# The second and third head pair turned by another engine, with a new start order, and a reordered last stage, in a kernel of attention and two expert layers

## The chip, the core and the metric

The kernel runs on one core of a Trainium2 chip. Its engines each work through a queue of their own and wait for each other through semaphores: TensorE (PE in the profile; its weight loads are PEld), VectorE (DVE), ScalarE (ACT), GpSimd (POOL) and SyncE (SP), which here issues DMAs. The metric is the device time of one execution in microseconds (us), the median of three runs.

## The reference

The kernel computes attention with a memory term, then a layer with x - tanh(x), then a layer with a softmax gate and a layer normalisation:

```
q, k, v: (4, 8, 576, 64)    M_prev: (4, 8, 64, 64)    z_prev: (4, 8, 64)    beta: (8)
scores = q @ k.T / 8, causal;  a = exp(scores - max) / (sum + 1e-9);  local = a @ v
q_p = where(q > 0, q, exp(q) - 1) + 1
mem = (q_p @ M_prev) / (q_p . z_prev + 1e-6)
x = sigmoid(beta) * mem + (1 - sigmoid(beta)) * local        -> (2304 tokens, 512)

h = x @ w_in (512 x 2048);  y = (h - tanh(h)) @ w_out

h = y @ w2_in (512 x 1024);  e = exp(h - max(h));  u = h * e / (sum(e) + 1e-9)
out = ((u - mean(u)) / sqrt(var(u) + 1e-6) * g_ln) @ w2_out  -> (2304, 512)
```

## The kernel before

**Attention.** The 32 heads are worked on in 16 pairs, the two heads of a pair in the lower and upper 64 partitions. For each pair q and k come from memory as rows of tokens and have to be turned, so that the 64 features lie on partitions. There are two ways. `load_n` (L183) fetches them in natural layout, `t_pe` (L203) turns them with 18 small matmuls on TensorE, and `t_cp` (L213) copies the result out of PSUM, on ScalarE for q and on VectorE for k. Or `_load` (L159) fetches each of them in four overlapping pieces of 32 partitions by 1120 numbers, and `q_t`, `k_t` (L241) turn them with one VectorE instruction (L245). The first three pairs (0 to 2) go the first way, all later ones the second.

With q and k turned, `s_r` (L303) computes the scores of a pair block by block, and `s_l` (L328) the scores of the last 64 tokens of two pairs together (S_L, issued with the odd pair). VectorE adds the mask and takes the maximum (`s_max`, L345, which appears as L353), ScalarE takes the exponential with its sum (`s_exp`), GpSimd scales (`s_norm`, L407), TensorE turns the probabilities (`a_t`), and `a_pv` multiplies by v into the PSUM tile X, which `a_mem` (L429) has opened with the memory term. The memory term itself takes `f_neg`, `f_exp`, `f_max` (the function of q) and `m_mm` (L279), `m_eps`, `m_inv`, `m_mul`. `g_exp`, `g_inv` (L119 to L121) compute the gate from beta.

The order of all these steps at the start is a table written out by hand, `PROLOGUE` (L516): each entry is a step, its pair, the engine (s SyncE, a ScalarE, v VectorE, p GpSimd) and a part; `run` (L579) issues them in that order. From pair 4 on `PERIOD` takes over, a table for two pairs. Since an engine works through its queue in order, the table's order is the order of each queue.

PSUM is shared: tag S has two tiles of 1024 columns in turn (scores, S_L, the memory product R, turned q and k, later H), T two of 512, X one.

**The two layers.** The first (Moe1) runs from about 190 to 590 us, with steps h and y alternating on TensorE. The second (Moe2) works on 18 blocks of 128 tokens, 0 to 17, in the loop at L1214. For block i:

- `y_split` (L1245): the block's y is split into a high half (ScalarE, L1246) and a low half (GpSimd, L1247) for products of full precision.
- `h_mm` (L919): H = y @ w2_in, 24 matmuls of 512 columns on TensorE.
- `top` (L930): the row maximum on VectorE. `exp` (L936): the exponential on ScalarE.
- `norm`: on VectorE L944 to L950 (sum, product, mean and variance), then the power -1/2 of the variance on GpSimd (L951), then the normalisation on VectorE (L958).
- `turn` (L960): blocks 1 to 16 are turned in 32x32 squares by VectorE (L964), written to memory (L966) and read back in four pieces (L969); this is the round trip. Blocks 0 and 17 are turned by TensorE instead (`t_parts`, L986, with the high half on ScalarE at L996 and the low half on VectorE at L1001).
- `spread` (L974): what came back is split into a high half (ScalarE, L979) and a low half (GpSimd, L980).
- `o_mm` (L1003): the product with w2_out, 24 matmuls, into PSUM tag X (blocks 0 to 14 and 16), S (15) or both (17); the products with the high half come first, those with the low half last. Then a copy out of PSUM on ScalarE (L1018) and the store. A tile O1X in the profile is the product of block 1 in tag X: it can start when O0X, in the same PSUM tile, has been copied out.

The loop issues `h_mm(i)` and the other steps of block i, and `o_mm(i - 3)` at its end. As the code stands there is an order by hand here too:

```
m2.h_mm(i); m2.y_split(i + 2); m2.top(i); m2.exp(i)
if i > 3: m2.spread(i - 2)
m2.norm(i); next(lo, None)          # lo: the low halves of block 0, at i == 1
if i == 3: m2.spread(1)
m2.turn(i)
if i > 2: m2.o_mm(i - 3)
```

Of the kernel before, what the change touches and what calls it, by code (L numbers as in the profile page):

```python
# [31 lines left out]
class Attention:  # L32
# [150 lines left out]
    def load_n(self, p, k):  # L183

        D, src = self.D, (self.q, self.k)[k]
        b, h0 = divmod(2 * p, self.H)
        if p == 1:
            t = self.ap.tile([P, self.poff[self.NC - 1]], F32, tag="P", name=f"N{p}_{k}", bufs=4)
        else:
            t = self.sp.tile([P, self.S * 2], F32, tag="nqnk"[2 * k : 2 * k + 2], name=f"N{p}_{k}", bufs=1)  # L190
# [325 lines left out]
    PROLOGUE = """  # L516
        load_n:0:s:0 load_n:0:a:1 load_v:0:s warm:0:- heat:0:-:8 load_g:0:- load_n:1:s:1
        t_pe:0:-:0 t_cp:0:a:0 load_n:1:s:0 f_neg:0:p load_m:0:- t_pe:0:-:1 t_cp:0:v:1 g_exp:0:-
        s_r:0:-:2 f_exp:0:- g_inv:0:- w_ld:2:- s_max:0:-:4 m_gate:0:- s_r:0:-:1 load_n:2:s:1
        s_exp:0:-:4 s_max:0:-:0 s_r:0:-:3 s_max:0:-:5 load_n:2:s:0 s_exp:0:-:5 s_max:0:-:7  # L520
        t_pe:1:-:0 s_exp:0:-:0 s_max:0:-:6 s_exp:0:-:7 t_pe:1:-:1 s_max:0:-:2 g_cpy:0:-
        s_exp:0:-:2 s_max:0:-:1 t_cp:1:v:1 t_cp:1:a:0 f_neg:1:p s_l:1:- s_exp:0:-:1 s_max:0:-:3
        s_exp:0:-:3 f_max:0:- s_exp:0:-:6 s_max:1:-:8 s_r:1:-:1 s_eps:0:-:1 s_exp:1:-:8
        s_eps:0:-:0 s_inv:0:-:1 s_norm:0:-:5 s_r:1:-:3 s_inv:0:-:0 s_max:1:-:9 f_exp:1:-
        s_norm:0:-:0 s_max:1:-:6 t_pe:2:-:0 load_q:3:s s_norm:0:-:4 s_exp:1:-:9 s_max:1:-:7
        s_norm:0:-:3 t_cp:2:a:0 s_r:1:-:2 s_max:1:-:1 s_max:1:-:3 s_norm:0:-:6 s_max:1:-:2
        s_exp:1:-:6 s_max:1:-:0 m_mm:0:- s_norm:0:-:2 s_max:1:-:5 s_exp:1:-:7 s_max:1:-:4
        s_norm:0:-:7 s_exp:1:-:0 a_t:0:-:0 m_eps:0:- f_max:1:- s_eps:1:-:0 s_exp:1:-:5
        t_pe:2:-:1 load_k:3:s m_inv:0:- a_ev:0:a:0 s_inv:1:-:0 s_norm:1:-:8 m_mul:0:-
        s_exp:1:-:4 a_t:0:-:4 a_ev:0:v:4 a_t:0:-:2 a_ev:0:a:2 s_norm:0:-:1 a_t:0:-:5  # L530
        s_norm:1:-:9 t_cp:2:v:1 a_t:0:-:1 a_ev:0:a:5 load_v:1:s s_norm:1:-:7 a_t:0:-:3
        a_ev:0:a:3 a_t:0:-:6 f_neg:2:p s_r:2:-:3 s_max:2:-:7 a_ev:0:a:6 s_exp:1:-:1 m_mm:1:-
        a_ev:0:a:1 f_exp:2:- s_max:2:-:6 s_r:2:-:1 s_exp:1:-:2 m_eps:1:- f_max:2:- s_exp:1:-:3
        s_eps:1:-:1 s_r:2:-:2 s_max:2:-:2 s_exp:2:-:7 s_max:2:-:1 a_mem:0:- s_inv:1:-:1
        s_norm:1:-:5 m_inv:1:- s_exp:2:-:2 s_max:2:-:3 a_pv:0:-:0 s_max:2:-:5 s_exp:2:-:5
        s_norm:1:-:1 s_max:2:-:4 s_norm:1:-:4 a_pv:0:-:1 s_max:2:-:0 m_mul:1:- s_exp:2:-:4
        s_norm:1:-:3 a_pv:0:-:3 s_exp:2:-:3 q_t:3:- s_norm:1:-:2 a_pv:0:-:2 s_exp:2:-:6
        s_norm:1:-:0 a_t:1:-:1 a_ev:1:a:1 x_ev:0:v s_norm:1:-:6 a_t:1:-:3 m_mm:2:- f_neg:3:p
        a_ev:1:a:3 k_t:3:- s_exp:2:-:1 a_t:1:-:0 s_exp:2:-:0 m_eps:2:- a_t:1:-:2 m_inv:2:-
        a_ev:1:a:0 m_mul:2:- s_eps:2:-:0 a_mem:1:- s_eps:2:-:1 a_ev:1:a:2 s_inv:2:-:0  # L540
        s_norm:2:-:7 a_t:1:-:4 s_inv:2:-:1 a_ev:1:a:4 s_l:3:- s_max:3:-:8 s_r:3:-:1 s_r:3:-:3
    """


# [733 lines left out]
```

## Time and profile before

| what | value |
| --- | --- |
| median of three runs | 799.09 us (798.41, 799.12, 799.09) |
| the profiled execution | 798.38 us |
| its span (first to last instruction) | 796.3 us |
| granted TensorE clock | 1.00 throughout |
| TensorE busy, share of the span | 783.3 us, 98% |
| weight loads | 698.5 us, 88% |
| VectorE | 571.1 us, 72% |
| ScalarE | 353.3 us, 44% |
| GpSimd | 373.6 us, 47% |

A share is a mean over stages. The same sums over a stretch show which engine is full there, and the timeline of an engine shows its groups of instructions in order, with the idle time ahead of a group and what ended it in square brackets.

### The profile page before, as it was taken

What the parts mean: (1) busy time and instruction counts of PE and PEld (TensorE: products, weight loads), DVE (VectorE), ACT (ScalarE), POOL (GpSimd) and SP (SyncE); (2) the same over time, 40 slices, a digit from 0 to 9 for tenths busy, and PEclk for the clock granted to TensorE, in tenths of its full rate; (3) what the DMA queues carried; (4) which work ended last, traced back from release to release, by engine and by line L of the source; (5) the groups of instructions that cost most, each with busy time, mean ns of one, the idle gap of its engine ahead of it and who ended that gap; (6) DMA issues with size and microseconds to landing.
All of it is one profiled execution on the core that took longest, in us unless ns stands there. A gap on an engine that the chain in (4) does not pass through costs nothing.

```text
span 796.3 us, 13582 instructions
## 1 busy us (share of the span) xinstructions
PE 783.3 (98%) x5040; PEld 698.5 (88%) x5040; DVE 571.1 (72%) x1102; ACT 353.3 (44%) x714; POOL 373.6 (47%) x390
## 2 busy tenths in 40 slices
PE   7999999999999999999999999999999899999997
PEld 5777777778999999999999999999998688888886
DVE  4899989884587767777777777756867776556650
ACT  5889999996233233332332333313322233332321
POOL 5788999979233233333332334312541444333421
PEclk9999999999999999999999999999999999999999
DMA  6577878731012121121211211211101344433341
GB/s 138 118 192 169 174 139 166 170 81 57 27 59 76 54 79 54 55 80 54 68 66 54 80 54 56 77 27 51 57 1 53 106 146 133 132 107 119 105 141 45
DMA packets 76418, 71.98 MB, mean 90 GB/s; under 512 B 50368, under 2 KB 58816, under 8 KB 76352
## 3 DMA queue, kind: packets, MB, share of 16 engines
q1 hardware_dynamic: 76192, 70.82, 32.6%
q8 instruction: 40, 0.66, 0.4%
q10 hardware_dynamic: 160, 0.30, 0.2%
q14 instruction: 26, 0.21, 0.1%
HBM read 53.26 MB, written 13.11 MB: 83 GB/s over the span
## 4 chain that ended last, share of the span: by engine, by line
PE 91%; DVE 4%; POOL 1%; DMA 1%; ACT 1%; issue 1%; SPq 0%; DVEq 0%; ACTq 0%
PE H L699 25%; PE Y L728 25%; PE H L919 10%; PE T L447 6%; PE X L474 5%; PE S L323 4%; PE R L279 2%; PE S_L L339 1%; PE X L429 1%; PE O16X L1013 1%; PE O10X L1013 1%; PE O7X L1013 1%; PE O4X L1013 1%; PE O13X L1013 1%; PE O12X L1013 1%; PE O11X L1013 1%
## 5 line engine op out<-in xcount | busy, mean ns | idle before, releaser
L728 PE MATMUL Y<-G,wo 128*128 128x384 f32 x1152 | 207.7, 335 | 0.0
L728 PEld LDWEIGHTS Y<-G,wo 128*128 128x128 f32 x1152 | 200.8, 188 | 0.1
L699 PE MATMUL H<-xh,wi 128*128 128x384 f32 x768 | 156.8, 337 | 0.0
L873 POOL TENSOR_TENSOR cvw<-cvw,cva 128x512 f32<-128x512 f32 x48 | 62.0, 1291 | 182.2 <-DVE cva L871 139.6
L699 PEld LDWEIGHTS H<-xh,wi 128*128 128x128 f32 x768 | 135.6, 188 | 0.4 <-issue 0.4
L712 ACT ACTIVATE t<-H 128x768 f32<-128x768 f32 x48 | 39.0, 813 | 211.6 <-PE H L699 211.6
L919 PE MATMUL H<-w2i,Ys 128*128 128x512 f32 x384 | 89.8, 390 | 0.0
L699 PE MATMUL H<-xT,wi 128*128 128x384 f32 x384 | 89.4, 336 | 0.0
L919 PEld LDWEIGHTS H<-w2i,Ys 128*128 128x128 f32 x384 | 72.1, 188 | 15.0
L713 DVE TENSOR_TENSOR t<-H,t 128x768 f32<-128x768 f32 x48 | 46.0, 957 | 52.1 <-ACT t L712 52.1
L407 POOL TENSOR_SCALAR P<-P,sm,og 128x512 f32<-128x512 f32 (+3 forms) x124 | 81.1, 666 | 3.5 <-DVE sm L396 1.4
L742 DVE TENSOR_TENSOR yT<-Y,yT 128x384 f32<-128x384 f32 (+1 forms) x126 | 78.9, 682 | 0.0
L715 DVE TENSOR_TENSOR G<-t,G 128x768 fp32r<-128x768 f32 x48 | 47.0, 980 | 42.3 <-ACT G L714 42.3
L380 ACT ACTIVATE P<-P,mx 128x384 f32<-128x384 f32 (+3 forms) x128 | 71.1, 557 | 4.6 <-DVE mx L353 4.3
L699 PEld LDWEIGHTS H<-xT,wi 128*128 128x128 f32 x384 | 68.6, 188 | 0.0
L714 ACT CAST G<-t 128x768 fp32r<-128x768 f32 x48 | 40.1, 835 | 50.9 <-DVE t L713 50.9
L353 DVE CUSTOM_DVE_ANT_0 P<-S,mask 128x384 f32<-128x384 f32 (+3 forms) x128 | 55.7, 484 | 8.6 <-PE S L323 8.4
L980 POOL TENSOR_TENSOR L<-rest,L 128x1024 fp32r<-128x1024 f32 x16 | 38.4, 2400 | 47.8 <-ACT L L979 46.2
L454 ACT COPY pt<-T 128x512 f32<-128x512 f32 (+1 forms) x95 | 53.6, 605 | 10.9 <-PE T L447 10.2
L474 PE MATMUL X<-pt,v 128*64 128x64 f32 (+4 forms) x576 | 47.3, 318 | 0.0
L474 PEld LDWEIGHTS X<-pt,v 128*64 128x64 f32 x576 | 26.4, 137 | 23.5 <-issue 19.8
L936 ACT ACTIVATE e<-H,s 128x1024 f32<-128x1024 f32 x18 | 20.1, 1116 | 59.6 <-DVE s L930 59.6
(280 smaller groups left out, 1234.3 us busy)
## 6 DMA issues: line engine op xcount, KB each, us to landing
raw<-in_moe_w_in_dram SPq DMA_DIRECT2D x24, 512.0 KB, 3.7
raw<-in_moe_w_out_dram SPq DMA_DIRECT2D x16, 512.0 KB, 3.4
D<-rest SPq DMA_DIRECT2D x16, 512.0 KB, 2.6
rest<-D SPq DMA_DIRECT2D x64, 128.0 KB, 2.9
q<-in_q_dram SPq DMA_DIRECT2D x52, 140.0 KB, 3.2
out_dram<-ob SPq DMA_DIRECT2D x17, 256.0 KB, 3.0
v<-in_v_dram SPq DMA_DIRECT2D x32, 128.0 KB, 3.5
xT<-x SPq DMA_DIRECT2D x16, 256.0 KB, 2.7
```

Source lines behind the costliest of these rows:

```text
L353: self.nc.vector.tensor_tensor_reduce(out=self._block(p, i), in0=s, in1=mask, scale=-0.125, scalar=3.0e38, op0=ALU.add, op1=ALU.min, accum ...
L380: self.nc.scalar.activation(t, t, AF.Exp, bias=self.mx[p][:, i : i + 1], scale=-1.0, accum_out=self.sm[p][:, i : i + 1],)
L407: eng.tensor_scalar(d, d, self.sm[p][:, i : i + 1], og, ALU.mult, ALU.mult)
L447: nc.tensor.transpose(T[:, P * i : P * i + P], t, self.ident)
L454: self.copy(pt, T)
L474: self.nc.tensor.matmul(self.X[j * D : (j + 1) * D, q0 : q0 + w], v[:, kb, j, :], pt[:, o : o + w], start=False, stop=False, skip_group_ch ...
L699: nc.tensor.matmul(H[a:z, f], wi[:, wl, c, f * P + a : f * P + z], self.x[n][xl][:, c], start=(count[f] == 0), stop=(count[f] == 3 * KD - ...
L728: nc.tensor.matmul(Y[d][:, 0:NB], wo[:, wl, f, d * P : (d + 1) * P], G[:, gl, f], start=(i == 0), stop=(i == 3 * KF - 1),)
L742: nc.vector.tensor_tensor(y, src, y, ALU.add)
L873: self.eng.tensor_tensor(w, w, a, ALU.add)
L919: nc.tensor.matmul(H[:, nh * 512 : (nh + 1) * 512], Y[:, yl, c, :], w2i[:, wl, c, nh * 512 : (nh + 1) * 512], start=(k == 0), stop=(k == 3 ...
L1013: nc.tensor.matmul(O[n][:, 0:w], L[:, ll, f, :], self.w2o[f][:, wl, a : a + w], start=(k == 0), stop=(k == len(order) - 1),)
```

## The change

**At the start.** q and k of pairs 1 and 2 go the second way: `load_q`, `load_k` with `q_t`, `k_t` on VectorE in place of `load_n`, `t_pe` and `t_cp`. The tiles of pair 1 lie in the buffers of tag P, as they did before. `heat`, which issues matmuls on the identity that nothing reads, writes to tag X instead of S; beside the eight at the start there are ten behind the scores of pair 0. v of pair 0 is loaded later. The rest of the table holds the same steps in another order, all the way to its end.

**In the last stage.** `y_split(i + 2)` comes behind the exponential, `spread(i - 2)` ahead of `norm`; `spread(1)` comes right behind `h_mm(3)`; the low halves of block 0 come behind `turn(1)`; the spread of block 16 comes ahead of `o_mm(15)`.

Line numbers behind L168 are higher by 2 or 3 in the changed kernel (L353 is L356, L979 is L982, L1246 is L1248).

```
         b, h0 = divmod(2 * p, self.H)
-        t = self.nat[name] = self.sp.tile([P, G, D], F32, tag=f"n{name}", name=f"{name}{p}", bufs=1)
+        if p == 1:
+            t = self.ap.tile([P, self.poff[self.NC - 1]], F32, tag="P", name=f"N{name}{p}", bufs=4)
+            t = t[:, 0 : G * D].rearrange("p (g d) -> p g d", d=D)
+        else:
+            t = self.sp.tile([P, G, D], F32, tag=f"n{name}", name=f"{name}{p}", bufs=1)
+        self.nat[name, p] = t
...
     def heat(self, p, n):
-        t = self.ps.tile([P, 1024], F32, tag="S", name="heat", bufs=2)
+        t = self.ps.tile([P, 1024], F32, tag="X", name=f"heat{p}")
...
     PROLOGUE = """
-        load_n:0:s:0 load_n:0:a:1 load_v:0:s warm:0:- heat:0:-:8 load_g:0:- load_n:1:s:1
+        load_n:0:s:0 load_n:0:a:1 heat:0:-:8 load_g:0:- warm:0:- t_pe:0:-:0 load_q:1:s t_cp:0:a:0
+        load_m:0:- f_neg:0:p t_pe:0:-:1 t_cp:0:v:1 load_k:1:s g_exp:0:- s_r:0:-:2 g_inv:0:-
+        load_k:2:s q_t:1:- f_neg:1:p s_r:0:-:1 s_r:0:-:3 heat:1:-:10 s_max:0:-:5 s_exp:0:-:5 load_q:2:s
...
         m2.h_mm(i)
+        if i == 3:
+            m2.spread(1)
+        m2.top(i)
+        m2.exp(i)
         if i + 2 < NTL:
             m2.y_split(i + 2)
-        m2.top(i)
-        m2.exp(i)
+        if i > 3:
+            m2.spread(i - 2)
         lo = iter(())
...
-        if i > 3:
-            m2.spread(i - 2)
         m2.norm(i, i in direct)
-        next(lo, None)
-        if i == 3:
-            m2.spread(1)
         if i not in direct:
             m2.turn(i)
+        next(lo, None)
         if i > 2:
             m2.o_mm(i - 3)
+    m2.spread(NTL - 2)
     m2.o_mm(NTL - 3)
-    m2.spread(NTL - 2)
```

VectorE's queue at the start, of the kernel before, from the last step of the gate on. P0 and S0 are blocks of probabilities and scores of pair 0, N1_1T is k of pair 1 as TensorE has turned it, f0 the function of q of pair 0; a row with mx alone reads out the maximum.

```order
L121 TENSOR_SCALAR og_143<-g_142 128x8
L353 ISA P0_0_212,mx0_210<-S0_2_201,mask_93 128x384
...
L353 ISA P0_1_229,mx0_210<-S0_11_216,mask_93 128x128
L353 ISA mx0_210 128x1
L219 COPY kT1_282<-N1_1T_258 128x9x64
L353 ISA P0_1_229,mx0_210<-S0_11_216,mask_93 128x256
L353 ISA mx0_210 128x1
L267 SCALAR_TENSOR_TENSOR f0_301<-qT0_168,e0_173 128x576
L353 ISA PL1_8_306,mx1_304<-S1_L0_288,maskL_94 128x576
```

The same place of the changed kernel, where Nq1 and Nk1 are q and k of pair 1 as they were loaded:

```order
L121 TENSOR_SCALAR og_137<-g_136 128x8
L248 STREAM_TRANSPOSE qT1_213<-Nq1_162 128x18x32
L356 ISA P0_1_239,mx0_237<-S0_2_202,mask_93 128x384
...
L356 ISA P0_1_239,mx0_237<-S0_3_223,mask_93 128x512
L356 ISA mx0_237 128x1
L248 STREAM_TRANSPOSE kT1_265<-Nk1_196 128x18x32
L270 SCALAR_TENSOR_TENSOR f0_270<-qT0_167,e0_173 128x576
L399 RECIPROCAL sm0_238<-sm0_238 128x6
L356 ISA PL1_8_287,mx1_285<-S1_L0_272,maskL_94 128x576
```

The copy of k of pair 1 out of PSUM has gone from between the score blocks of pair 0; two turns have come in, q ahead of all eight blocks and k behind all eight.

ScalarE's queue in the last stage, of the kernel before, from the split of block 4 on. Ys is a high half of y, e2 an exponential, L a high half of what came back from memory, ob a copy of a product.

```order
L1246 CAST Ys4_6601<-yT_2936 128x512
L936 ACTIVATE e2_2_6606,s2_2_6604<-H2_2_6576,s2_2_6604 128x1024
L1246 CAST Ys5_6649<-yT_2936 128x512
L936 ACTIVATE e2_3_6654,s2_3_6652<-H2_3_6624,s2_3_6652 128x1024
L979 CAST L1_6665<-rest_6429 128x1024
L1018 COPY ob0_0_6700<-O0X_6675 128x512
L1246 CAST Ys6_6728<-yT_2936 128x512
L936 ACTIVATE e2_4_6733,s2_4_6731<-H2_4_6703,s2_4_6731 128x1024
L979 CAST L2_6735<-rest_6429 128x1024
L1018 COPY ob1_0_6779<-O1X_6754 128x512
```

The same place of the changed kernel:

```order
L939 ACTIVATE e2_2_6546,s2_2_6544<-H2_2_6519,s2_2_6544 128x1024
L1248 CAST Ys4_6548<-yT_2879 128x512
L982 CAST L1_6592<-rest_6372 128x1024
L939 ACTIVATE e2_3_6597,s2_3_6595<-H2_3_6567,s2_3_6595 128x1024
L1248 CAST Ys5_6599<-yT_2879 128x512
L1021 COPY ob0_0_6643<-O0X_6618 128x512
L939 ACTIVATE e2_4_6673,s2_4_6671<-H2_4_6646,s2_4_6671 128x1024
L1248 CAST Ys6_6675<-yT_2879 128x512
L982 CAST L2_6678<-rest_6372 128x1024
L1021 COPY ob1_0_6722<-O1X_6697 128x512
```

Each split of y stands behind the exponential that it stood ahead of, and the spread of block 1 ahead of the exponential of block 3.

GpSimd's queue at the same place, of the kernel before; s2 with 128x1 is the power, L a low half of what came back from memory.

```order
L1247 TENSOR_TENSOR Ys2_6508<-yT_2936,Ys2_6508 128x512
L1247 TENSOR_TENSOR Ys3_6536<-yT_2936,Ys3_6536 128x512
L951 TENSOR_TENSOR s2_0_6455<-s2_0_6455,nhalf_2945 128x1
L882 TENSOR_TENSOR w2o_c_6176<-cvw_6420,w2o_c_6176 128x512
L951 TENSOR_TENSOR s2_1_6539<-s2_1_6539,nhalf_2945 128x1
L1247 TENSOR_TENSOR Ys4_6601<-yT_2936,Ys4_6601 128x512
L951 TENSOR_TENSOR s2_2_6604<-s2_2_6604,nhalf_2945 128x1
L1247 TENSOR_TENSOR Ys5_6649<-yT_2936,Ys5_6649 128x512
L951 TENSOR_TENSOR s2_3_6652<-s2_3_6652,nhalf_2945 128x1
L980 TENSOR_TENSOR L1_6665<-rest_6429,L1_6665 128x1024
```

The same place of the changed kernel:

```order
L1249 TENSOR_TENSOR Ys2_6451<-yT_2879,Ys2_6451 128x512
L954 TENSOR_TENSOR s2_0_6398<-s2_0_6398,nhalf_2888 128x1
L1249 TENSOR_TENSOR Ys3_6483<-yT_2879,Ys3_6483 128x512
L885 TENSOR_TENSOR w2o_c_6119<-cvw_6363,w2o_c_6119 128x512
L954 TENSOR_TENSOR s2_1_6479<-s2_1_6479,nhalf_2888 128x1
L1249 TENSOR_TENSOR Ys4_6548<-yT_2879,Ys4_6548 128x512
L954 TENSOR_TENSOR s2_2_6544<-s2_2_6544,nhalf_2888 128x1
L983 TENSOR_TENSOR L1_6592<-rest_6372,L1_6592 128x1024
L1249 TENSOR_TENSOR Ys5_6599<-yT_2879,Ys5_6599 128x512
L954 TENSOR_TENSOR s2_3_6595<-s2_3_6595,nhalf_2888 128x1
```

The power of block 0 has one split ahead of it instead of two, and the low half of block 1 has moved ahead of the power of block 3.

## Rows read from the trace of the kernel before

**Rows 1.** The page's first line.

```profile
span 796.3 us, 13582 instructions
```

**Rows 2.** Stretch, length, busy us of PE PEld DVE ACT POOL, clock, DMA share, GB/s.

```profile
10.00:30.00 20.00, 18.36 (x241) 13.02 (x239) 14.79 (x49) 16.57 (x43) 12.73 (x20) 1.00 0.57 137
30.00:590.00 560.00, 559.71 (x3813) 515.43 (x3813) 431.44 (x865) 274.82 (x576) 284.15 (x302) 1.00 0.32 82
600.00:640.00 40.00, 36.77 (x161) 29.60 (x160) 31.16 (x43) 11.41 (x19) 13.72 (x11) 1.00 0.26 86
640.00:779.00 139.00, 139.00 (x609) 114.03 (x608) 84.30 (x130) 41.63 (x62) 51.31 (x36) 1.00 0.39 125
```

**Rows 3.** Timeline, TensorE, last stage: start, duration, instruction, count, [idle before, releaser].

```profile
624.24 1.19 PE L1013 MATMUL O1X<-w2o,L 128*128 128x512 f32 x4 [2.13 <-ACT ob L1018]
...
629.30 0.73 PE L1013 MATMUL O1X<-w2o,L 128*128 128x512 f32 x2 [1.10 <-POOL L L980]
```

**Rows 4.** Timeline, TensorE, near the end.

```profile
781.49 1.19 PE L1013 MATMUL O16X<-w2o,L 128*128 128x512 f32 x4 [0.79 <-ACT L L979]
```

**Rows 5.** Timeline, TensorE, the start.

```profile
12.11 1.26 PE L209 MATMUL N_0T<-ident,N 64*64 64x64 f32 x36
...
15.60 1.69 PE L339 MATMUL S_L<-kT,qT 64*64 64x512 f32 x16 [0.79 <-ACT qT L219]
...
22.08 1.35 PE L279 MATMUL R<-MZ,f 128*128 128x130 f32 x10 [0.37 <-POOL P L407]
...
32.21 0.76 PE L429 MATMUL X<-ident,xm 128*128 128x128 f32 x5
```

**Rows 6.** Timeline, VectorE, the start.

```profile
10.78 0.56 DVE L353 CUSTOM_DVE_ANT_0 P<-S,mask 128x384 f32<-128x384 f32 x1 [0.47 <-PE S L323]
...
14.85 1.19 DVE L219 COPY kT<-N_1T 128x576 f32<-128x576 f32 x1 [0.81 <-PE N_1T L209]
```

**Rows 7.** Line L245: durations min/median/max in ns, first and last start.

```profile
L245 DVE STREAM_TRANSPOSE qT<-q x13: 1222/1246/1252, 34.6 to 162.0; 128x576 f32<-128x576 f32 x13
```

**Rows 8.** Timeline, SyncE's queue, the start.

```profile
10.73 1.63 SPq L140 DMA_DIRECT2D MZ<-in_M_prev_dram  x1
```

**Rows 9.** Line L181, the loads of q and k in four pieces.

```profile
L181 SPq DMA_DIRECT2D q<-in_q_dram x52: 328/420/1379, 20.7 to 155.9; - x52
...
DMA to landing us min/median/max: 2.4/3.2/4.4
```

**Rows 10.** Timeline, ScalarE, last stage.

```profile
621.56 1.11 ACT L936 ACTIVATE e<-H,s 128x1024 f32<-128x1024 f32 x1 [7.89 <-DVE s L930]
...
623.60 0.59 ACT L1018 COPY ob<-O0X 128x512 f32<-128x512 f32 x1
```

**Rows 11.** Timeline, VectorE, last stage.

```profile
617.29 1.77 DVE L958 TENSOR_SCALAR e<-e,s 128x1024 f32<-128x1024 f32 x1 [0.66 <-POOL s L951]
...
620.26 1.19 DVE L930 TENSOR_REDUCE s<-H 128x1 f32<-128x1024 f32 x1
...
757.84 1.23 DVE L930 TENSOR_REDUCE s<-H 128x1 f32<-128x1024 f32 x1 [2.17 <-PE H L919]
```

**Rows 12.** Line L958: durations min/median/max in ns, first and last start.

```profile
L958 DVE TENSOR_SCALAR e<-e,s x16: 811/814/2843, 606.7 to 764.6; 128x1024 f32<-128x1024 f32 x16
```

**Rows 13.** Timeline, GpSimd, last stage.

```profile
594.49 2.54 POOL L1247 TENSOR_TENSOR Ys<-yT,Ys 128x512 fp32r<-128x512 f32 x2 [4.07 <-ACT Ys L1246]
...
617.22 1.29 POOL L1247 TENSOR_TENSOR Ys<-yT,Ys 128x512 fp32r<-128x512 f32 x1
```

**Rows 14.** Timeline, TensorE, H of block 1.

```profile
593.59 5.74 PE L919 MATMUL H<-w2i,y 128*128 128x512 f32 x24
```

**Rows 15.** Timeline, SyncE's queue, the round trip of block 1.

```profile
610.85 0.35 SPq L966 DMA_DIRECT2D D<-rest  x1
613.62 1.75 SPq L969 DMA_DIRECT2D rest<-D  x4
```

**Rows 16.** Line L969, landing of the reads of the round trip.

```profile
DMA to landing us min/median/max: 2.5/2.9/4.4
```

More of the change, by code (lines that the diff above doesn't have):

```diff
@@ L186, in load_n @@
         b, h0 = divmod(2 * p, self.H)
[L187 to L190, printed above, removed]
+        t = self.sp.tile([P, self.S * 2], F32, tag="nqnk"[2 * k : 2 * k + 2], name=f"N{p}_{k}", bufs=1)
         t = self.nat[p, k] = t[:, 0 : self.S].rearrange("p (g d) -> p g d", d=D)
@@ L246, in _transposed @@
             t.rearrange("d (g p) -> d g p", p=Q) if blocks
-            else t.rearrange("d (p g) -> d g p", p=Q), self.nat.pop(name)[:, :, 0:Q]
+            else t.rearrange("d (p g) -> d g p", p=Q), self.nat.pop((name, p))[:, :, 0:Q]
         )
@@ L516 @@
     PROLOGUE = """
-        load_n:0:s:0 load_n:0:a:1 load_v:0:s warm:0:- heat:0:-:8 load_g:0:- load_n:1:s:1
[L518 to L540, printed above, removed]
@@ L541 @@
-        s_norm:2:-:7 a_t:1:-:4 s_inv:2:-:1 a_ev:1:a:4 s_l:3:- s_max:3:-:8 s_r:3:-:1 s_r:3:-:3
+        load_n:0:s:0 load_n:0:a:1 heat:0:-:8 load_g:0:- warm:0:- t_pe:0:-:0 load_q:1:s t_cp:0:a:0
+        load_m:0:- f_neg:0:p t_pe:0:-:1 t_cp:0:v:1 load_k:1:s g_exp:0:- s_r:0:-:2 g_inv:0:-
+        load_k:2:s q_t:1:- f_neg:1:p s_r:0:-:1 s_r:0:-:3 heat:1:-:10 s_max:0:-:5 s_exp:0:-:5 load_q:2:s
+        s_max:0:-:1 s_max:0:-:4 s_max:0:-:0 s_exp:0:-:4 s_max:0:-:2 m_gate:0:-
+        s_max:0:-:3 s_exp:0:-:1 w_ld:2:- s_max:0:-:6 s_exp:0:-:3 s_max:0:-:7 g_cpy:0:-
@@ new lines @@
+        s_exp:0:-:0 f_exp:0:- k_t:1:- s_exp:0:-:2 s_eps:0:-:1 s_exp:0:-:6 f_max:0:- s_l:1:-
+        s_exp:0:-:7 s_eps:0:-:0 s_inv:0:-:1 s_max:1:-:8 s_exp:1:-:8 s_r:1:-:1 s_norm:0:-:0
+        s_norm:0:-:4 s_max:1:-:9 s_r:1:-:3 s_norm:0:-:5 s_max:1:-:1 s_max:1:-:0 s_exp:1:-:0
+        s_inv:0:-:0 s_r:1:-:2 s_max:1:-:7 s_norm:0:-:3 s_exp:1:-:9 s_max:1:-:6 m_mm:0:-
+        s_norm:0:-:7 f_exp:1:- q_t:2:- load_q:3:s s_norm:0:-:2 s_exp:1:-:7 s_norm:0:-:6
+        s_max:1:-:2 s_exp:1:-:6 a_t:0:-:0 s_max:1:-:4 s_eps:1:-:0 a_ev:0:a:0 s_max:1:-:3
@@ new lines @@
+        a_t:0:-:2 s_norm:0:-:1 m_eps:0:- s_inv:1:-:0 s_max:1:-:5 s_norm:1:-:8 a_t:0:-:4
+        a_ev:0:a:2 load_v:0:s m_inv:0:- m_mul:0:- a_t:0:-:5 s_exp:1:-:1 s_norm:1:-:9 s_exp:1:-:5
+        k_t:2:- a_t:0:-:3 f_neg:2:p a_ev:0:a:5 a_t:0:-:6 load_k:3:s a_ev:0:a:6 s_r:2:-:3
+        a_ev:0:v:4 f_max:1:- s_exp:1:-:4 s_norm:1:-:6 a_t:0:-:1 s_max:2:-:7 a_ev:0:a:3 m_mm:1:-
+        load_v:1:s a_ev:0:a:1 s_max:2:-:6 s_exp:1:-:3 s_r:2:-:1 s_exp:1:-:2 s_eps:1:-:1
+        s_max:2:-:1 s_exp:2:-:7 s_r:2:-:2 s_max:2:-:0 s_inv:1:-:1 s_norm:1:-:1 f_exp:2:-
@@ new lines @@
+        m_eps:1:- a_mem:0:- m_inv:1:- s_max:2:-:3 s_norm:1:-:3 a_pv:0:-:0 s_max:2:-:4
+        s_norm:1:-:7 s_max:2:-:2 s_max:2:-:5 s_exp:2:-:5 a_pv:0:-:2 s_norm:1:-:5 f_max:2:-
+        a_pv:0:-:1 s_norm:1:-:2 m_mul:1:- s_exp:2:-:1 a_pv:0:-:3 s_exp:2:-:2 s_norm:1:-:0
+        q_t:3:- a_t:1:-:3 s_exp:2:-:6 s_norm:1:-:4 a_t:1:-:1 s_exp:2:-:3 f_neg:3:p m_mm:2:-
+        x_ev:0:v a_ev:1:a:3 s_exp:2:-:4 k_t:3:- a_t:1:-:0 a_ev:1:a:1 a_mem:1:- s_eps:2:-:0
+        m_eps:2:- a_ev:1:a:0 a_t:1:-:4 m_inv:2:- m_mul:2:- a_t:1:-:2 s_exp:2:-:0 s_eps:2:-:1
@@ L542 @@
+        a_ev:1:a:4 s_inv:2:-:1 s_l:3:- a_ev:1:a:2 s_inv:2:-:0 s_norm:2:-:7 s_max:3:-:8 s_r:3:-:1
+        s_r:3:-:3
     """
```

## The prediction

> **What bounds the kernel now.** I read the page's first part, then the busy time by stretch, then the timeline of the stretches in which TensorE idles. The span is 796.3 us [rows 1]. From 30 to 590 us TensorE is busy 559.71 of 560 us, and from 640 to 779 all of it, at a granted clock of 1.00, which is the 2.4 GHz level [rows 2]; there the reader is to see that no other engine is as full. So an edit pays only where TensorE waits, or where TensorE itself gets less to do: in 10:30, where it idles 1.64 us, in 600:640, where it idles 3.23 [rows 2] in two waits of 2.13 and 1.10 us [rows 3], and at a wait of 0.79 us near the end [rows 4]. The change touches these places and no others.
>
> **The first stage.** Four turns leave TensorE (q and k of the second and third pair, 18 matmuls each). One takes 1.26 us [rows 5], four 5.0. Two copies leave ScalarE and two leave VectorE, at 1.19 us [rows 6]; four VectorE turns of 1.25 us come in [rows 7]: 4 x 1.25 - 2 x 1.19 = 2.6 us more for VectorE.
>
> What decides is when the second pair's scores S_L begin; they began at 15.60 [rows 5]. I follow VectorE. Up to the gate values nothing changes for it; it was done with them at 10.31 and waited 0.47 us for the first scores, which it took at 10.78 [rows 6]. Now it turns q of the second pair first, 10.31 + 1.25 = 11.56, and is 0.8 late from here. Seven score blocks of the first pair stood between 10.78 and 14.04 (14.85 less the 0.81 of idle time ahead of the copy [rows 6]): 3.26, and the eighth, of 256 columns, took 0.35 more. In the new order all eight follow without a break: 11.56 + 3.6 = 15.2. Then k of the second pair is turned, 1.25: 16.4, and S_L begins there, 0.8 later than before.
>
> From S_L to the first product of pair 0 with X, at 32.21 [rows 5], 16.6 us went by, in which two turns of the third pair stood (1.35 and 1.26). Without them and with no new wait it takes 14.0, and X begins at 30.4: 1.8 us gained. That is one end. The other is a loss: VectorE now carries its turns of the third pair (2.5 us, for one copy of 1.2) between the scores that TensorE waits to have emptied; if all of these 1.3 us and the 0.8 reach TensorE and none of the 2.6 us saved is usable, it is 2.1 us lost. VectorE idles 5.21 us of 10:30 [rows 2], twice what it gains in work, which speaks for the gaining end; but it is the engine that TensorE follows there. I take 0.6 us gained, nearer to no change than to the full end.
>
> The loads must hold for this. Of each of these q and k the new layout fetches four pieces of 140 KB, where two of 144 KB stood: twice the bytes. On SP's queue k of the second pair stands behind q of the first, the gate, the four pieces of q, a small table and the memory tensors. That makes 16 issues; one of the memory tensors at 1.63 us [rows 8] and 15 at the 0.42 of such a piece [rows 9] take 7.9, and I add 2 us for those that take longer than a piece and for the queue's own waits: the last goes out at about 10. With a landing of 3.2 us, 4.4 at most [rows 9], it is there at 13.2 to 14.4. It is wanted at 15.2: covered, by a microsecond at the worst; what comes later than that, the start loses. The values v of pair 0 now go out behind q of the fourth pair, which waits for VectorE's turn of q of the third. I put that turn at about 22, an estimate (16.4, then S_L and about six blocks of scores): v lands near 27 and is wanted after 30.4, so this costs nothing, until that turn is 3 us later.
>
> Ten dummy matmuls come in behind the first pair's scores. Ten real ones make two of the rows of 1.35 us (five of 130 columns each, 0.27 us apiece [rows 5]), so these take 2.7 us, and lie between 12.1 and 16.4, where TensorE would else stand still: no cost. By the rows such gaps do not take the clock down: TensorE idles 2.13 us before O1X [rows 3] and the granted clock of 600:640 is 1.00 [rows 2]. The Trainium skill (TensorE: Matmul & The Clock Gate, HAM oscillation) speaks against the change here: gaps in TensorE's work can bring the throttle back, so that what follows runs at 1.2 GHz. By the rows the sum stands, by the rule the 1.69 us of S_L would double, and what follows as well (rival D).
>
> **The last stage.** The spread of block i-2 (ScalarE writes the high half, L979, then GpSimd the low half, L980) now stands ahead of the normalisation, the split of y (L1246, L1247) behind the exponential, and the turn of block 1 ahead of block 0's low halves (L1001).
>
> O1X waited 2.13 us for the copy of O0X at 623.60, which was queued on ScalarE behind the exponential of block 3 at 621.56 and a spread [rows 10]. The exponential waited for VectorE's row maximum at 620.26 [rows 11], and that was late by VectorE's own queue. For blocks 1 and 2 the normalisation L958 took 1.76 and 1.77 us (the second is shown [rows 11]), where its median is 0.81 [rows 12]; a split of y on GpSimd began 0.07 us ahead of each (617.22 against 617.29 [rows 11, 13]). In the new order no split follows the power on GpSimd, but it waits for the next exponential. That gives 0.95 twice. And the power of block 0 stood behind two splits, 2.54 us together [rows 13], now behind one; of these 1.27 us about 0.7 are usable, since H of block 1 ends at 599.33 and its maximum stood at about 600.1 [rows 14]. So the maximum of block 3 starts at 620.26 - 1.9 - 0.7 = 617.7, the exponential at 619.0, the split of y follows it (0.6), and the copy of O0X ends at 621.4. TensorE is done with H of block 4 at 622.1 (624.24 - 2.13 [rows 3]): the wait is gone.
>
> The spread of block 1 needs its round trip through memory: out at 610.85, back by four reads issued from 613.62 on over 1.75 us [rows 15], each landing 2.9 us after issue, 4.4 at most [rows 16]. Out moves to 607.9 (0.95 + 0.7 earlier, and 1.28 more as L1001 stands behind the turn), so all is back between 615.0 and 616.4, the high half done by 617.5, the low half (2.4 us) by 620. TensorE wants it from about 626 (622.1 and the 3.96 us from O1X's start to its second wait at 628.20 [rows 3]): the 1.10 us go too.
>
> One thing is open. L958 of block 2 now starts at 617.29 - 1.65 = 615.6, and GpSimd's low half of block 1 can start from 616.0: a case that no row shows, since in all of them GpSimd was first. By the nearest rows it costs 0 to 2.0 us (0.81 against 2.84 at most [rows 12]); with 2.0 the copy of O0X would end at 623.4 and TensorE wait 1.3. I take 0: VectorE starts first. The Trainium skill (SBUF — State Buffer, Who interferes with whom) says that whichever of the two engines starts first holds the shared port for its whole instruction. By it the extra is 0 here, by the worst row 2.0 and the time 1.3 us more.
>
> The 0.79 us: the high half of block 16 (L979) was queued on ScalarE behind the copy of O15S, and moves ahead of it. A round trip takes some 7 us (610.85 to 613.62 + 1.75 + 2.9 [rows 15, 16]), and block 16's set out a whole round ahead, so the data is there. O16X then follows its transposes directly: 0.79 gained.
>
> In every later round the power on GpSimd waits at most one split longer than before, 1.27 us. VectorE idles 2.17 us per round ahead of its maximum [rows 11]: covered, with 0.9 left.
>
> **Sum.** 0.6 + 2.13 + 1.10 + 0.79 = 4.6 us. The profiled execution took 798.4 (its span and 2.1 us around it), so 793.8 for it. The median of the runs is 0.7 above that execution, at 799.1, which gives 794.5; I take 794.3.
>
> **Rivals.**
> A. L958 of block 2 collides with the low half as above, or the round trip lands late, so that O1X still waits 1.3 to 1.6 us: 3.0 to 3.3 gained, 796.0. For it: the two starts lie 0.4 us apart. Against: VectorE is first.
> B. The start loses: k of the second pair lands late, or VectorE's turns come in the way of the scores. The lower end of the first stage, -2.1, with 4.0 from the end: 1.9 gained, 797.2. For it: twice the bytes on one queue, and TensorE follows VectorE there. Against: 5.21 us of idle time of VectorE [rows 2].
> C. Slower: on GpSimd the split, the spread and the power now stand in one row behind the exponential. If that lengthens VectorE's round by more than its 2.17 us of idle time [rows 11], each of some 13 rounds loses the excess; this is the point from which it decides. With 1.27 for the later power and 2.03 for a colliding L958 (2.84 - 0.81 [rows 12]) in each round the excess is 1.1, in all 15 us, and the time 809. Against: GpSimd can start nothing behind the power until the next exponential.
> D. The clock falls to 1.2 GHz in the gap before S_L. S_L alone costs 1.7 us more, all the work up to X 14: 796 to 808. Against: the 2.13 us at full clock.
>
> **How the numbers follow.** Forecast (both places pay) 0.66, A 0.15, B 0.12, C 0.03, D 0.04. The likeliest is 794.3. Its own range is 793 to 796; A and most of B reach to 797, and the gaining end of the first stage (1.2 more) to 793: 792.5 to 797.0. About 0.2% (1.6 us) is what a measurement of this kernel can tell from no change. Faster, under 797.5: the forecast, A, and over half of B: 0.88. Within 0.2%: the rest of B and part of D, 0.08. Slower: C and the rest of D, 0.04.
>
> **What would show it.** Right: S_L near 16.4 and X near 31.5 at the start; no idle time of TensorE before O1X, before its low half, and before O16X; L958 at 0.81 in every round; the copy of O0X done before H of block 4. Wrong: TensorE idle behind 30 us where it was not; L958 over 1 us; k of the second pair landing after 15; a granted clock under 1.00 in 10:30. The forecast falls if O1X still waits, or if X begins after 32.2.

## The result, and the profile after

The changed kernel takes 791.24 us (median of four runs, 790.76 to 791.69), the kernel before 798.76 beside it: a ratio of 0.9906, 95% interval 0.9889 to 0.9923. That is 7.5 us faster where 4.6 were forecast, and 1.3 us under the lower end of the range. The profiled execution took 791.37 us, 7.0 under the profiled one of before (798.38). One execution of e5 below (1213.84 us, granted clock 0.60) and one of e11 (2006.05 us) stand far outside all others and are left out.

The page's first line and the busy time by stretch of the changed kernel (stretch, its length, then busy us of PE, PEld, DVE, ACT and POOL, clock, DMA share, GB/s) answer to [rows 1, 2]:

```profile
span 789.6 us, 13348 instructions
```

```profile
10.00:30.00 20.00, 18.85 (x134) 12.56 (x134) 18.01 (x60) 16.12 (x47) 13.90 (x21) 1.00 0.85 193
...
600.00:640.00 40.00, 40.00 (x177) 32.86 (x176) 29.79 (x47) 12.85 (x22) 16.71 (x13) 1.00 0.34 112
640.00:779.00 139.00, 139.00 (x613) 114.08 (x612) 80.40 (x123) 40.50 (x62) 51.02 (x37) 1.00 0.37 119
```

TensorE waits no more in 600:640, where it idled 3.23 us. In 10:30 VectorE is busy 18.01 us instead of 14.79: it took 3.2 us more work out of its 5.21 us of idle time.

To see where the 6.7 us of span went, I cut it at three marks on TensorE: the first scores, the first product with X, and the first matmul of O16X. Five rows of the kernel before that stand in no group yet, from the timeline of TensorE (start, duration, instruction, count, idle before and its releaser; LDWEIGHTS is the weight load of a matmul):

```profile
9.71 2.43 PE L323 MATMUL S<-kT,qT 64*128 64x384 f32 x16 [1.37 <-DVE og L119]
...
16.09 0.20 PEld L339 LDWEIGHTS S_L<-kT,qT 64*64 64x64 f32 x7 [0.31 <-DVE kT L219]
...
17.22 2.17 PE L323 MATMUL S<-kT,qT 64*128 64x256 f32 x12
...
610.97 1.10 PE L1013 MATMUL O0X<-w2o,L 128*128 128x512 f32 x4
...
774.16 1.09 PE L1013 MATMUL O15S<-w2o,L 128*128 128x512 f32 x4
```

The same view of the changed kernel, start and last stage, against [rows 3 to 5, 14]:

```profile
9.99 2.43 PE L326 MATMUL S<-kT,qT 64*128 64x384 f32 x16 [1.37 <-DVE og L119]
12.35 2.50 PE L204 MATMUL heat<-ident 128*128 128x128 f32 x20
14.77 2.42 PE L342 MATMUL S_L<-kT,qT 64*64 64x512 f32 x16
17.12 2.69 PE L326 MATMUL S<-kT,qT 64*128 64x256 f32 x16
20.63 1.35 PE L282 MATMUL R<-MZ,f 128*128 128x130 f32 x10 [0.81 <-issue]
...
30.03 0.77 PE L432 MATMUL X<-ident,xm 128*128 128x128 f32 x5
...
591.35 5.74 PE L922 MATMUL H<-w2i,y 128*128 128x512 f32 x24
...
608.73 1.10 PE L1016 MATMUL O0X<-w2o,L 128*128 128x512 f32 x4
...
614.27 5.61 PE L922 MATMUL H<-w2i,Ys 128*128 128x512 f32 x24
619.72 1.10 PE L1016 MATMUL O1X<-w2o,L 128*128 128x512 f32 x4
...
623.43 0.62 PE L1016 MATMUL O1X<-w2o,L 128*128 128x512 f32 x2
...
768.17 1.09 PE L1016 MATMUL O15S<-w2o,L 128*128 128x512 f32 x4
...
774.47 1.18 PE L1016 MATMUL O16X<-w2o,L 128*128 128x512 f32 x4
```

| | first scores | to X | X to O16X | O16X to the end | span |
| --- | --- | --- | --- | --- | --- |
| before | 9.71 | 22.50 | 749.28 | 14.8 | 796.3 |
| after | 9.99 | 20.04 | 744.44 | 15.1 | 789.6 |
| difference | +0.28 | -2.46 | -4.84 | +0.3 | -6.7 |

So 2.5 us come from the start (0.6 forecast) and 4.8 from the last stage (4.0 forecast). The first column follows the landing of the first loads. With the start of before it lay between 9.55 and 10.52 in three profiles (before, e1, e8), with the changed start between 9.99 and 10.33 (after, e2, e6), so its difference is chance here.

VectorE of the changed kernel at the start, the wait of its queue (DVEq, durations in ns) for k of the second pair with the landing of the four pieces of that k, and two pieces of the chain of waits (start, duration, what) answer to [rows 6, 7, 9]:

```profile
10.31 1.26 DVE L248 STREAM_TRANSPOSE qT<-Nq 128x576 f32<-128x576 f32 x1
11.41 0.54 DVE L356 CUSTOM_DVE_ANT_0 P<-S,mask 128x384 f32<-128x384 f32 x1
...
14.70 1.25 DVE L248 STREAM_TRANSPOSE kT<-Nk 128x576 f32<-128x576 f32 x1
...
17.23 0.76 DVE L356 CUSTOM_DVE_ANT_0 PL<-S_L,maskL 128x576 f32<-128x576 f32 x1 [0.35 <-PE S_L L342]
```

```profile
L248 DVEq EVENT_SEMAPHORE  x2: 21/965/1909, 12.5 to 12.5; - x2
...
DMA to landing us min/median/max: 3.0/3.1/4.4
```

```profile
14.78 1.18 DVE kT L248
...
16.00 0.34 PE S_L L342 x4
```

S_L begins at 14.77 although k of the second pair is turned only at 15.95: its first part uses the first pair's q and k. The part that needs the new k runs from 16.00. In the kernel before it was the same: S_L began at 15.60, and the part of the second pair waited for VectorE's copy of k until 16.09. TensorE goes on to the next scores at 17.12, where it did at 17.22 before.

VectorE of the changed kernel in the last stage, its line L961 (durations in ns), GpSimd and ScalarE answer to [rows 10 to 13]:

```profile
613.47 0.81 DVE L961 TENSOR_SCALAR e<-e,s 128x1024 f32<-128x1024 f32 x1 [0.66 <-POOL s L954]
...
615.48 1.19 DVE L933 TENSOR_REDUCE s<-H 128x1 f32<-128x1024 f32 x1
```

```profile
L961 DVE TENSOR_SCALAR e<-e,s x16: 811/812/816, 603.7 to 758.6; 128x1024 f32<-128x1024 f32 x16
```

```profile
614.21 2.41 POOL L983 TENSOR_TENSOR L<-rest,L 128x1024 fp32r<-128x1024 f32 x1 [0.78 <-ACT L L982]
```

```profile
616.79 1.12 ACT L939 ACTIVATE e<-H,s 128x1024 f32<-128x1024 f32 x1 [2.65 <-DVE s L933]
...
618.40 0.58 ACT L1021 COPY ob<-O0X 128x512 f32<-128x512 f32 x1
```

L958, now L961, takes 0.81 us, the maximum of block 3 stands at 615.48 and the copy of O0X at 618.40: 4.8 and 5.2 us earlier than before, of which 2.2 are the start's.

### The profile page after: what moved, and what is told of

It reads as the page before. It is cut to its first block, busy times and chain, and to the rows that moved or that the text cites. A ratio compares the mean times of both kernels' runs of the same rounds, so it can differ in the third digit from the quotient of the medians.

```text
span 789.6 us, 13348 instructions
## 1 busy us (share of the span) xinstructions
PE 781.2 (99%) x4916; PEld 697.0 (88%) x4916; DVE 567.4 (72%) x1104; ACT 349.6 (44%) x712; POOL 373.9 (47%) x390
## 4 chain that ended last, share of the span: by engine, by line
PE 96%; DVE 2%; DMA 1%; SPq 1%; issue 0%; ACTq 0%; ACT 0%; DVEq 0%
PE H L702 25%; PE Y L731 25%; PE H L922 12%; PE T L450 6%; PE X L477 5%; PE S L326 4%; PE R L282 2%; PE X L432 1%; PE S_L L342 1%; DVE P L356 1%; PE O13X L1016 1%; PE O9X L1016 1%; PE O6X L1016 1%; PE O3X L1016 1%; PE O0X L1016 1%; PE O12X L1016 1%
## 5 line engine op out<-in xcount | busy, mean ns | idle before, releaser
L1249 POOL TENSOR_TENSOR Ys<-yT,Ys 128x512 fp32r<-128x512 f32 x16 | 20.8, 1301 | 94.6 <-ACT Ys L1248 82.2
L356 DVE CUSTOM_DVE_ANT_0 P<-S,mask 128x384 f32<-128x384 f32 (+3 forms) x128 | 55.8, 483 | 7.0 <-PE S L326 6.9
```

The lines of the kernel that those rows point to most:

```text
L356: self.nc.vector.tensor_tensor_reduce(out=self._block(p, i), in0=s, in1=mask, scale=-0.125, scalar=3.0e38, op0=ALU.add, op1=ALU.min, accum ...
```

## Experiments

All times are medians beside runs of the kernel before on the same chip; "to X" and "X to O16X" are the columns above. The theory after the result: the start gives 2.2 to 2.5 us because TensorE is freed of 2.6 us of turns and VectorE has the room; the last stage gives 4.8, because each wait costs more than its idle time in the row. The rival: the forecast's sizes are right and the rest is an interaction or the clock.

**Each half alone.** e1 takes the start of before with the changed loop of the last stage, e2 the changed start with the old loop:

```
e1:  PROLOGUE, _load, load_n, heat as before;   loop over blocks as changed
e2:  PROLOGUE, _load, load_n, heat as changed;  loop over blocks as before
```

> The start of the kernel before with the last stage of the changed one. Theory (each of the three waits of TensorE cost about 0.25 us more than its idle time in the row, so the last stage alone gives 4.8 us): from the first matmul of H of block 1 to the first of O16X it takes 183.1 us, as in the changed kernel (187.9 before); first product with X at 32.2 as before; time 4.8 under the kernel before. Rival (the waits cost what the rows say, 4.0, and the rest of the gain comes from the start reaching into the last stage): 183.9 us, 4.0 under.

> The start of the changed kernel with the last stage of the kernel before. Theory (the start alone gives 2.2 us): first product with X at 30.0, O1X waits 2.1 and 1.1 us and O16X 0.8 as before, 187.9 us from H of block 1 to O16X, time 2.2 under the kernel before. Rival (the forecast's 0.6, the rest being the last stage's): X at 31.6, 0.6 under.

e1: 793.27, ratio 0.9935 (0.9921 to 0.9948), 5.2 us under the 798.44 of before. To X 22.42, X to O16X 744.47; from H of block 1 (593.33) to O16X (776.44) 183.1 us, as the theory had it. e2: 796.48, ratio 0.9972 (0.9962 to 0.9982), 2.0 under. To X 20.04, X to O16X 749.22, with all three waits as before. The two add to 7.1 of the 7.5 us, and in the traces (to X and X to O16X) to 7.4 of 7.3: no interaction shows.

**The turns without the new order.** e3 keeps the table of before and exchanges only the steps of pairs 1 and 2 (last stage as before):

```
-  load_n:1:s:1 ... load_n:1:s:0 ... t_pe:1:-:0 ... t_pe:1:-:1 ... t_cp:1:v:1 t_cp:1:a:0
+  load_k:1:s   ... load_q:1:s   ...                               k_t:1:-    q_t:1:-
   (pair 2 alike; no second heat)
```

> The second kernel of this set, but with the start table of before, in which only the loads of the second and third pair and their turns on VectorE stand in the places of the old loads and copies (no dummy matmuls added). Theory (the turns that leave TensorE pay by themselves, whatever the order): X at 30 to 30.6, 1.6 to 2.2 us under the kernel before. Rival (the new order pays): the two turns of the second pair stand between two score blocks, the second pair's part of S_L begins at 16.3 instead of 15.95 or later, TensorE waits, and X begins at 31.5 or later; at most 0.7 under, or above.

799.8, ratio 1.0019 (1.0011 to 1.0028): slower than before, to X 23.66. The theory falls in its first form; the order decides. TensorE of e3, and its stretches (columns as above):

```profile
13.71 1.07 PE L342 MATMUL S_L<-kT,qT 64*64 64x512 f32 x2 [0.36 <-DVE mx L356]
16.51 1.66 PE L342 MATMUL S_L<-kT,qT 64*64 64x512 f32 x12 [1.74 <-DVE qT L248]
18.10 3.59 PE L326 MATMUL S<-kT,qT 64*128 64x256 f32 x16
```

```profile
16.00:17.00 1.00, 0.49 (x7) 0.21 (x9) 1.00 (x4) 0.24 (x1) 0.37 (x1) 1.00 1.01 197
...
18.00:19.00 1.00, 1.00 (x8) 0.81 (x6) 0.69 (x3) 0.07 (x1) 0.74 (x3) 0.50 1.02 229
19.00:20.00 1.00, 1.00 (x8) 0.80 (x8) 0.88 (x6) 0.89 (x3) 0.71 (x2) 0.50 1.01 229
```

Two things go wrong. VectorE turns k and q back to back between two score blocks, so that TensorE waits 1.74 us; and behind that gap the granted clock falls to 0.50, the 1.2 GHz level: the twelve matmul records of S_L take 1.66 us and the sixteen of S 3.59, where e11 below, in the same order at a clock of 1.00, has 1.19 and 3.10. This is the forecast's rival D, in another kernel. The rule of the Trainium skill cited in the forecast (TensorE: Matmul & The Clock Gate, HAM oscillation: gaps in TensorE's work bring the throttle back) agrees with this trace.

**The same with dummy matmuls.** e5, and e11, which is the same kernel and whose profile is read (`heat` writes to tag X in both, as in the changed kernel):

```
-  s_r:0:-:3 s_max:0:-:5
+  s_r:0:-:3 heat:1:-:10 s_max:0:-:5
```

> The third kernel (old order, turns of the second and third pair on VectorE in place) with the ten dummy matmuls of the changed kernel behind the last scores of pair 0. In the third kernel TensorE stood idle for 1.74 us ahead of the second pair's part of S_L, and its granted clock fell to 0.50 from 17 to 20.7 us; from its first scores to the first product with X it took 23.66 us (22.5 in the kernel before, 20.04 in the changed one). Theory (the clock took some 1.3 us of that, VectorE's order the rest): clock 1.00, 22.3 us, time about that of the kernel before (within 0.5). Rival (the clock was all of it): 20.0 us, and 2 us under the kernel before. Second rival (the clock falls all the same): 23.5.

> The fifth kernel (old order, turns on VectorE in place, ten dummy matmuls) once more for a profile at full clock: its time was 799.0, 0.8 under the same without the dummy matmuls and equal to the kernel before. Theory (VectorE's order holds TensorE even where the clock stays): granted clock 1.00 in 10:30, from the first scores to X 22.3 to 23 us. Rival (the clock still falls): below 0.95 in 10:30 and over 23 us.

e5 took 798.95 us (ratio 1.0008, 1.0000 to 1.0017), e11 798.63 (1.0005, 0.9996 to 1.0015): no gain over before. In the profile of e11 the clock is 1.00 in 10:30 and it is 22.31 to X, as the theory had it. So of the 3.62 us between e3 and the changed start about 1.35 were the clock and 2.27 the order. TensorE of e11:

```profile
17.00 1.19 PE L342 MATMUL S_L<-kT,qT 64*64 64x512 f32 x12 [0.78 <-DVE qT L248]
18.12 3.10 PE L326 MATMUL S<-kT,qT 64*128 64x256 f32 x16
...
25.59 0.66 PE L450 MATMUL T<-ident,P 128*128 128x128 f32 x4 [1.03 <-ACT pt L457]
26.68 0.76 PE L450 MATMUL T<-ident,PL 128*128 128x128 f32 x5 [0.44 <-POOL PL L410]
```

The time that the turns freed on TensorE went into waits for the other three engines, which still worked in the old order.

**The new order without the third pair's turns.** e9 is the changed kernel, with pair 2 back on TensorE:

```
-  load_k:2:s   ... load_q:2:s   ... q_t:2:-                                   ... k_t:2:-
+  load_n:2:s:1 ... load_n:2:s:0 ... (behind s_max:1:-:5) t_pe:2:-:0 t_cp:2:a:0 ... t_pe:2:-:1 t_cp:2:v:1
```

> The changed kernel, but the third pair's q and k are loaded in natural layout and turned by TensorE with copies on ScalarE and VectorE again (two turns of 1.3 us back on TensorE between S_L and the first product with X, 1.3 us less for VectorE). Theory (what leaves TensorE there is gained in full, since VectorE has the room): from the first scores to X 22.6 us instead of 20.04, at least 21.8 if the turn fills the 0.81 us of idle time before R; time 1.8 to 2.6 above the changed kernel. Rival (VectorE sets the pace there, and its 1.3 us less pays for TensorE's more): 20.0 to 20.8 us, time within 0.8.

794.04 (ratio 0.9945, 0.9932 to 0.9959), 2.7 us above the changed kernel; to X 23.05 instead of 20.04. The two turns cost 3.0 us, their own 2.5 and more; VectorE's 1.3 us less bought nothing. TensorE of e9:

```profile
23.36 1.26 PE L212 MATMUL N_0T<-ident,N 64*64 64x64 f32 x36 [0.53 <-DVE mx L356]
...
25.97 1.26 PE L212 MATMUL N_1T<-ident,N 64*64 64x64 f32 x36 [0.22 <-ACT qT L222]
```

Beside their 1.26 us the turns wait 0.53 and 0.22 us, by their releasers for a PSUM tile of tag S, which the score blocks and the copies hold. So the turns in the old order bring little (22.31 against 22.50 before), and the new order with half of them nothing (23.05); together they give 20.04. The new order with all turns on TensorE was not run, nor another place for the two turns of e9.

**The dummy matmuls.** e4 and e7 leave out `heat:1:-:10`, e10 doubles it (`heat:1:-:20`); e6 is the changed kernel once more.

> The changed kernel without the ten dummy matmuls behind the first pair's scores. Theory (they fill time in which TensorE waits for VectorE's turn of k at 15.95, and cost nothing): pair 0's part of S_L begins near 13, the second pair's part at 15.95 as with them, X at 30.0, granted clock 1.00, time the same within 0.2 us. Rival (they hold the clock up): granted clock under 1.00 in 10:30, S_L takes up to 1.7 us longer and X begins at 31.7 or later. Second rival (they are in the way of S_L): X earlier by up to 1 us.

> The changed kernel once more, beside the next one on one chip: 791.2, X 20.04 us behind the first scores, granted clock 1.00 or 0.999 in every execution.

> The changed kernel without the ten dummy matmuls once more. The first time it was 1.2 us above the changed kernel, three of five executions had a mean granted clock of 0.998, and the profiled one, at 1.000, lost its 1.2 us at 89 us, where q of a later pair landed 1 us late. Theory (without them the clock falls in some executions, and that is the loss): mean clock 0.998 in about half of the executions, which are 1 us or more above those at 1.000, and those are within 0.5 us of the changed kernel. Rival (the late q is the loss and belongs to the kernel): late q again in the profile, all executions 1.2 above. Third (chance): no difference.

> The changed kernel with twenty dummy matmuls behind the first pair's scores in place of ten. Ten end just as S_L's first part may begin, and the second pair's part waits for VectorE's turn of k till 1.2 us later. Theory (the cover is 1.2 us, the next ten take 2.5): S_L begins at once behind them, without the wait inside it, and ends 1.8 us later; X 1.3 to 1.9 us later behind the first scores (21.3 to 21.9). Rival (TensorE has room there): X at 20.0 to 20.3.

e6 took 791.36; e4 792.43 (ratio 0.9924, 0.9912 to 0.9937) and e7 792.05 (0.9916, 0.9904 to 0.9929), which is 0.7 to 1.2 above the changed kernel, with no execution of e7 as fast as the slowest of e6 (791.72 against 791.60). In both profiles it is 20.04 to X, at a clock of 1.00. TensorE of e7, then of e10:

```profile
13.03 1.07 PE L342 MATMUL S_L<-kT,qT 64*64 64x512 f32 x2 [0.30 <-DVE mx L356]
15.16 2.36 PE L342 MATMUL S_L<-kT,qT 64*64 64x512 f32 x14 [1.06 <-DVE mx L356]
```

```profile
12.29 4.73 PE L204 MATMUL heat<-ident 128*128 128x128 f32 x40
16.95 1.20 PE L342 MATMUL S_L<-kT,qT 64*64 64x512 f32 x16
```

Without them TensorE idles instead, and S_L ends at the same distance from the first scores (17.44 - 10.30 = 7.14, and 17.12 - 9.99 = 7.13 with them): they cost nothing. With twenty, S_L runs through in 1.20 us and ends 1.0 us later; X is 1.04 later (21.08), the time 792.46. I expected 1.3 to 1.9, from the 1.69 us that S_L took before, a wait included. What the ten are worth is not shown by a profile. The mean granted clock was 0.998 in five of the nine executions of e4 and e7, and 0.999 or 1.000 in all eight of the changed kernel and e6; in e7 the two at 0.998 took 792.15 and 792.52 us, the two at 0.999 791.72 and 791.95. That fits e7's theory of a short fall of the clock in some executions, but the profiled ones show none at the start. The late q of e4's profile (VectorE waited 0.98 us for it at 89 us) did not come back in e7, so it was chance. So the clock is the likelier cause of the 0.7 to 1.2 us, but it is not shown.

**One edit of the last stage.** e8 is the kernel before, with only

```
-        if i + 2 < NTL: m2.y_split(i + 2)
         m2.top(i); m2.exp(i)
+        if i + 2 < NTL: m2.y_split(i + 2)
```

> The kernel before with one edit: the split of y stands behind the exponential. Theory (VectorE was late by GpSimd's splits): L958 at 0.81 us in blocks 1 and 2, the copy of O0X some 2.5 us earlier, the first wait of O1X at most 0.3 us; the low half of block 1 still stands behind the power of block 3 on GpSimd, so the second wait stays at 1 to 1.5; O16X as before; from H of block 1 to O16X 185.9 to 186.3 us (187.9 before), time 1.6 to 2 under. Rival (the spread of block 1 ahead of the copy is what holds O1X): the first wait stays above 1.5, 187.5 or more.

796.14 (ratio 0.9963, 0.9950 to 0.9976), 2.6 us under before. From H of block 1 (594.34) to O16X (779.59) 185.25 us, against 187.90: 2.65 gained, more than the 1.6 to 2.0 expected, since the second wait shrank too (0.59 instead of 1.10). VectorE, GpSimd and TensorE of e8:

```profile
616.34 0.81 DVE L958 TENSOR_SCALAR e<-e,s 128x1024 f32<-128x1024 f32 x1 [0.67 <-POOL s L951]
...
625.05 2.86 DVE L958 TENSOR_SCALAR e<-e,s 128x1024 f32<-128x1024 f32 x1 [0.73 <-POOL s L951]
```

```profile
624.99 2.38 POOL L980 TENSOR_TENSOR L<-rest,L 128x1024 fp32r<-128x1024 f32 x1
```

```profile
622.87 1.19 PE L1013 MATMUL O1X<-w2o,L 128*128 128x512 f32 x4
...
627.42 0.72 PE L1013 MATMUL O1X<-w2o,L 128*128 128x512 f32 x2 [0.59 <-POOL L L980]
```

L958 of blocks 1 and 2 is at 0.81, and the 2.13 us of wait before O1X are gone: GpSimd's splits were what made VectorE late. In block 3, where GpSimd's low half starts 0.06 us ahead of L958, it still takes 2.86. The other edits of the last stage were not run one by one: they give the step from e8's 185.25 us to the 183.12 of the changed kernel together.

## Why the prediction was wrong

**The places** were right: all the gain lies in the start, at O1X and at O16X.

**The step that failed** is "What decides is when the second pair's scores S_L begin", and the choice that rested on it, "I take 0.6 us gained, nearer to no change than to the full end". S_L does not wait for the second pair as a whole: its first part is the first pair's. The forecast set the start of the whole S_L before, 15.60, against the start of the second pair's part after, 16.4, and so found a delay of 0.8. That part began at 16.09 before and at 16.00 after: there is no delay. What counts is the end of S_L, which came 0.4 us earlier behind the first scores (7.13 against 17.22 - 9.71 = 7.51). From there to X it took 12.91 us instead of 14.99, so 2.08 of the 2.61 us of turns were gained: nearly the full end, for which I had 1.8 in all, S_L's delay taken off. The measured 2.46 lies beyond both of my ends. The reading against it, that TensorE follows VectorE there, was not false: it is what e3 and e11 show. But VectorE had 5.21 us of idle time and an order written to use it, and that view, which I read and then gave less than half its weight, came true; e11 and e9 show that the room alone would not have done it.

**The second mis-sized term** is the three waits, "2.13 + 1.10 + 0.79", 4.02 in all; they gave 4.78 from H of block 1 to O16X (187.90 to 183.12). From O0X to O1X (610.97 before, 608.73 after) it takes 2.28 us less, from O1X to its low half 1.35 less (5.06 to 3.71), from O15S to O16X 1.03 less (7.33 to 6.30); 0.12 lie elsewhere. So the three waits cost 0.15, 0.25 and 0.24 us beyond the idle time of their rows. The idle time leaves out what a wait does to its neighbours: the group behind the first two waits is shorter without them (1.10 us instead of 1.19, 0.62 instead of 0.73), and a group that nothing holds starts before the one ahead of it has ended by its row (H of block 4 ends at 614.27 + 5.61 = 619.88, O1X starts at 619.72). e1 repeats the sum.

**The loads** were covered, as said, but by luck. The last piece of k of the second pair went out at about 10, as forecast, and landed 4.4 us later: VectorE's queue waited for it from 12.5 on for 1.909 us, until 14.4, while the score blocks ahead of it ran, and the turn began at 14.70. That is the late end of the forecast's 13.2 to 14.4, and k was wanted half a microsecond earlier than the 15.2 forecast; so some 0.3 us was left of the microsecond. In the same start of e2 and e6 no piece took more than 3.3 us to land.

**The dummy matmuls** took 2.50 us (2.7 forecast), and were hidden, as said; e10 shows where the cover ends.

**The last stage** went as worked out: with the start's 2.2 us taken off, the maximum of block 3 was forecast at 615.5 (615.48 measured) and the end of the copy of O0X at 619.2 (618.98). L961 takes 811 to 816 ns in all sixteen blocks. Rival A fell: VectorE's normalisation ran from 613.47 to 614.28, GpSimd's low half began at 614.21, and neither was longer. But the two overlapped by only 0.07 us, so this hardly puts the case "VectorE first" to the test. GpSimd first is e8's block 3: GpSimd took its usual 2.38 us and VectorE 2.86 instead of 0.81. The rule of the Trainium skill cited in the forecast (SBUF — State Buffer, Who interferes with whom) agrees with that. Rivals B, C and D did not come; no round lost time (640:779 is full). The argument against D, the 2.13 us at full clock, holds for the one profiled execution and not in general: in e11 the clock falls behind the same wait, as the last section shows.

**The range** had at its lower end the gaining end of the start, sized too small, and waits at their face value. Start and last stage were each right in sign and short by 1.9 and 0.8 us. Between the profiled executions the gain is 7.0 us, between the medians 7.5; the forecast started from the median, and the last section says what may lie between the two.

## What to carry to other kernels

Work that moved from a full engine to one with idle time paid here only together with an order in which that engine reaches it in time: the move alone took 22.3 us to X and the order with half the move 23.05, against 22.5 before, and both together 20.0. Price a wait of TensorE by the distance between the starts of the groups around it, not by its idle time alone. And for a composite product such as S_L, look up which of its parts needs the late operand before a delay is put on the whole.
